# A new hand-written order for gated linear attention with an MLP: two late transposes on TensorE instead of one, one transfer transpose less, 119 fillers dealt out anew

## The chip, the cores and the metric

The kernel runs on one core of a Trainium2 chip. The core has five engines that run side by side, each through its own queue in order: TensorE (PE in the profile; PEld is its loading of weights), VectorE (DVE), ScalarE (ACT), GpSimd (POOL) and SyncE (SP), which here only issues transfers. The metric is the device time of one execution in microseconds. The profile's span, from the first to the last instruction, is a little shorter than that time.

## What is computed

Four batches, 8 heads, 768 steps, head size 48. A state of 48 x 48 complex numbers per head is turned and damped at each step by a gate, takes in the product of k and v, and is read with q. The result, laid out as 384 columns, goes through a LayerNorm, a two-layer MLP with ReLU (384 to 1536 to 384) and a residual.

```python
mag = np.sqrt(a_re * a_re + a_im * a_im)
scale = np.minimum(mag, 0.999) / (mag + 1e-06)
a_re_n, a_im_n = (a_re * scale, a_im * scale)
for t in range(S):
    ar, ai = (a_re_n[:, :, t, :, None].copy(), a_im_n[:, :, t, :, None].copy())
    new_re = ar * S_re - ai * S_im
    new_im = ar * S_im + ai * S_re
    kv = np.einsum('bhd,bhe->bhde', k[:, :, t], v[:, :, t])
    S_re, S_im = (new_re + kv, new_im)
    y[:, :, t] = np.einsum('bhd,bhde->bhe', q[:, :, t], S_re)
...
xn = (x - mu) / np.sqrt(var + 1e-06) * g_ln
ch = np.maximum(xn @ w_ch1, 0.0) @ w_ch2
return (x + ch).astype(np.float32)
```

## The kernel before

The recurrence is worked in chunks of 128 steps. Two neighbouring chunks form a pair; there are 12 pairs (P = 0 to 11, three to a batch) and 24 chunks (n = 2P and 2P + 1). Within a chunk the gates' logarithms and angles are summed up over the steps by a matmul with a triangle of ones, exponentials and sines of the sums scale q and k, and then the chunk is ordinary masked attention plus a carried state.

Each operation has a name, and the program has two parts. The function `pair_ops` (from line 397) only declares the operations: what each emits, which others it needs, which buffers it uses. The order is not worked out by anything: it is written by hand in a table, `PLAN` (line 39). A token is `name:engine`, with the number of the PSUM bank behind the engine where it writes one (`th.5.0:A`, `ph.5.0:P4`), and sometimes `@other`, which makes it wait until `other`, an operation of another engine, is done; line 208 calls this taking turns at the shared port, and it is used on POOL alone. `Graph.run` (line 162) emits the operations in the order of the table. So each engine's queue is the table read for that engine alone, and an operation that waits holds up everything behind it on its engine.

The names, by pair and chunk, with their lines:

- On the gates: `are`, `aim` load the two parts (449). `ln` and `iv` (452, 454) are a logarithm and an exponential of are on ACT; `r` (456) is the ratio aim/are on DVE or POOL; `r2` (460) its square, on ACT, DVE or POOL; `u` (466) the logarithm of 1 + r2 on ACT; `l` and `lc` (469, 473) sum and clip on DVE; `th` (489) the arctangent on ACT.
- The sums over steps on PE: `dec` (477, matmuls on 481) from `lc`, and `ph` (492, 507; pair 0 on 511 and 515) from `th` and from `car` (522), the angle carried from the pair ahead.
- From these on ACT: `e`, `en` (484, exponentials of dec), `sin` (533), `cos` (544, 556). `tab.log` and `tab.trig` (815) load one or the other table of functions into ACT.
- The factors: `ke`, `qe` (562) and `ks`, `qs` (572) are products on DVE or POOL.
- The transposes of ks and qs, one for each chunk, reach `ksT` and `qsT` in one of two ways (line 610 to 631): on PE (`kT`, `qT`, eight matmuls with the identity, line 613) and a copy from PSUM on DVE or ACT, or by a transfer that transposes, issued by SP (line 618). Where the table puts `ksT.n:S`, there is no `kT.n`.
- The attention: `am` (636) the scores, `atm` (644) the mask, `gm` and `G` (657, 673) the carried state, `y` (683) the output, `x` (695) its copy.
- The MLP: `bn` and `rstd` (698, 720) the statistics, `xtr` and `xT` (704, 711) the transpose of x, `mm1` (737), `relu` (752), `mm2` (771), `oa` and `ot` (779, 784), and `st` (796) the store. `wl.0` to `wl.5` (367) load the weights through POOL's queue, `wp` (386) and `wc` (391) fold LayerNorm's mean and gain into the first weight matrix. `v` (413) is a cast of the loaded `vf`.
- `dps`, `decc` (589, 599) bring the chunk's total decay to where the state needs it.

Pair 0 is cut into two halves of four heads each (`PARTS`), so its operations have a last index 0 or 1 and 384 columns instead of 768.

The fillers `warmw` (512 columns) and `warm` (256 columns) are matmuls whose results nobody reads; 119 of them stand in the table up to the first chunks' attention. They give PE something to run where it would wait for the gates.

Of the kernel before, what the change touches and what calls it, by code (L numbers as in the profile page):

```python
# [44 lines left out]
k.1.0:S warmw.12:P0 warmw.13:P0 warmw.14:P0 warmw.15:P0 warmw.16:P0 warmw.17:P0 warmw.18:P0 warmw.19:P0 warm.0:P0
warm.1:P0 warm.2:P0 warm.3:P0 warm.4:P0 warm.5:P0 warm.6:P0 warm.7:P0 warm.8:P0 warm.9:P0 warm.10:P0 warm.11:P0
warm.12:P0 warm.13:P0 warm.14:P0 warm.15:P0 warm.16:P0 warm.17:P0 warm.18:P0 dec.0.1:P5 en.0.1:A5 e.0.1:A5 iv.2.0:A
q.1.1:S l.1.0:V lc.1.0:V warm.19:P0 warm.20:P0 warm.21:P0 warm.22:P0 warm.23:P0 warm.24:P0 warm.25:P0 warm.26:P0
warm.27:P0 warm.28:P0 warm.29:P0 dps.0:P5 dec.1.0:P1 q.1.0:S pad.e.1:G@lc.0.0 are.3.0:S en.1.0:A1 vf.0.0:S
cmean:G@l.1.0 decc.0:V5 r.2.0:V wl.1:G e.1.0:A1 warm.30:P0 warm.31:P0 warm.32:P0 warm.33:P0 warm.34:P0 warm.35:P0  # L50
warm.36:P0 warm.37:P0 warm.38:P0 warm.39:P0 warm.40:P0 warm.41:P0 warm.42:P0 warm.43:P0 warm.44:P0 dps.1:P7 qrow:G
r2.2.0:V vf.0.1:S ke.0.0.0:V u.2.0:A wgc:V pad.ks.1:G@uth aim.3.0:S tab.trig.1:A qe.0.1.0:V th.0.1:A l.2.0:V car0.1:G
k.1.1:S warm.45:P0 warm.46:P0 warm.47:P0 warm.48:P0 warm.49:P0 warm.50:P0 warm.51:P0 warm.52:P0 warm.53:P0 warm.54:P0
warm.55:P0 warm.56:P0 warm.57:P0 warm.58:P0 warm.59:P0 warm.60:P0 warm.61:P0 warm.62:P0 warm.63:P0 ph.0.1:P2
qe.0.0.0:V th.0.0:A pad.ks.0:G ke.0.1.0:V pad.qs.1:G@ke.0.0.0 sin.0.1:A2 qs.0.1.1:V car.0.1:A2 ph.0.0:P5 vf.1.1:S
k.2.1:S vf.1.0:S are.4.0:S q.2.1:S warm.64:P0 warm.65:P0 warm.66:P0 qt.0.1:P2 th.1.0:A lc.2.0:V wl.0:G car.0.0:V5
sin.0.0:A5 wp.1:P3 decc.1:V7 ks.0.1.1:V warm.67:P0 warm.68:P0 warm.69:P0 warm.70:P0 qt.0.0:P5 wc.1.1:V3 ks.0.0.1:V
cos.0.1:A2 ph.1.0:P6 th.2.0:A ke.1.0.0:G@qs.0.1.1 wc.1.0:V3 wc.1.2:V3 sin.1.0:A6 qe.1.0.1:G cos.0.0:A5 warm.71:P0
warm.72:P0 warm.73:P0 warm.74:P0 warm.75:P0 warm.76:P0 warm.77:P0 warm.78:P0 warm.79:P0 warm.80:P0 warm.81:P0
# [1 line left out]
q.2.0:S qs.0.1.0:V ln.3.0:A wc.0.0:V1 wc.0.1:V1 qe.1.0.0:G qs.1.0.1:G@car.1.0 e.2.0:A4 ksT.0:A3 wl.2:G@car.1.0
iv.3.0:A warm.83:P0 warm.84:P0 warm.85:P0 warm.86:P0 warm.87:P0 warm.88:P0 warm.89:P0 warm.90:P0 warm.91:P0 warm.92:P0
warm.93:P0 warm.94:P0 warm.95:P0 warm.96:P0 qT.1:P5 qT.0:P2 v.0:G wc.0.2:V1 qsT.0:V2 qsT.1:V5 qt.1.0:P6 kT.1:P3
k.2.0:S tab.trig.3:A am.0:P0 ksT.1:V3 warm.97:P2 ph.2.0:P4 atm.0:V0 cos.1.0:A6 ke.1.0.1:G@qsT.0 r.3.0:G am.1:P2
gm.0:P7 sin.2.0:A4 y.0:P6 qt.2.0:P4 atm.1:V2 qs.1.0.0:V ks.1.0.0:V ks.1.0.1:V G.0:A7 gm.1:P7 x.0:A6 cos.2.0:A4
warm.98:P1 xtr.0:P0 r2.3.0:A y.1:P3 qT.3:P1 qT.2:P5 xT.0:V0 kT.3:P2 x.1:A3 qsT.3:V1 qsT.2:A5 kT.2:P3 th.3.0:A
tab.log.4:A xtr.1:P0 wl.3:G@qsT.3 ksT.3:V2 wp.2:P6 xT.1:V0 v.1:G@xT.1 ksT.2:V3 am.3:P4 u.3.0:A G.1:V7 ln.4.0:A
mm1.0.0.1:P0 ke.2.0.1:G@ksT.2 gm.2:P7 mm1.0.0.0:P0 aim.4.0:S G.2:A7 atm.3:V4 mm1.0.1.1:P2 wc.2.0:V6 qe.2.0.1:G@atm.3
wc.2.1:V6 am.2:P4 qe.2.0.0:G wc.2.2:V6 vf.2.1:S relu.0.0:A0 pad.ks.2:G@wc.2.0 are.5.0:S atm.2:V4 wl.4:G@wc.2.1
mm1.0.1.0:P2 gm.3:P7 relu.0.1:A2 q.3.1:S vf.2.0:S q.3.0:S iv.4.0:A y.3:P6 x.3:V6 ke.2.0.0:G k.3.0:S G.3:V7 ph.3.0:P0  # L70
y.2:P2 car.3.0:V0 mm1.0.2.1:P4 x.2:A2 xtr.3:P3 qs.2.0.1:V xT.3:V3 r.4.0:G@car.3.0 bn.1:V wl.5:G k.3.1:S xtr.2:P7
xT.2:A7 mm1.0.2.0:P4 mm1.1.1.0:P2 mm1.1.1.1:P2 tab.trig.5:A sin.3.0:A0 relu.1.1:A2 aim.6.0:S relu.0.2:V4 mm1.1.2.1:P6
bn.0:V mm1.1.2.0:P6 are.6.0:S qs.2.0.0:V mm2.0.0:P5 aim.5.0:S abs.3.0:A0 l.3.0:V r2.4.0:V lc.3.0:V th.4.0:A
mm1.1.0.0:P3 qT.4:P0 qT.5:P1 mm2.0.1:P5 cos.3.0:A relu.1.2:V6 qsT.5:V1 ks.2.0.1:G@r2.4.0 bn.3:V mm2.1.0:P2 vf.3.0:S
# [772 lines left out]
```

## Time and profile before

| | |
|---|---|
| time, median of 3 runs (lowest to highest) | 188.53 us (188.46 to 189.46) |
| time of the profiled execution | 188.47 us |
| its span | 186.8 us |
| granted TensorE clock, mean | 1.00 |
| transfers in the span | 36.98 MB, 198 GB/s on average |

How such a profile is read: busy times are sums over the span for each engine. A timeline row gives the start, how long the instruction (or a run of like ones) takes, the engine, the line of the kernel, what it writes and reads, and, in brackets, how long the engine had been idle before it and what ended that. A row of the groups gives a count, the busy time and mean time of one, and the idle time before them. The chain of waits is followed back from the last instruction, and tells at each moment which engine's work or which wait set the end. SPq is SP's queue of transfers; a transfer's time runs from its issue to its landing.

### The profile page before, as it was taken

The numbers are of one execution on the slowest core, as the hardware profiler recorded it, in microseconds if no ns is written. First come the engines' busy times: TensorE is split into PE (matmuls) and PEld (weight loads), VectorE is DVE, ScalarE is ACT, GpSimd is POOL, SyncE is SP. The second block draws the span as 40 slices with busy tenths as digits, with TensorE's granted clock in tenths as the row PEclk, the third lists the DMA queues.
The fourth block names the chain that finished last, engine by engine and source line by source line (L and its number), as shares of the span: only waits on it lengthen the run. The fifth ranks groups of instructions, "written<-read, shape, count | busy, mean of one in ns | idle before, by whom it ended". The sixth has DMA issues, their size and how long they took to land.

```text
span 186.8 us, 5174 instructions
## 1 busy us (share of the span) xinstructions
PE 179.2 (96%) x2046; PEld 138.6 (74%) x2048; DVE 154.4 (83%) x277; ACT 158.9 (85%) x225; POOL 120.3 (64%) x131
## 2 busy tenths in 40 slices
PE   5999999999999999999999999999999999799992
PEld 2488777887777889667877887878868778587771
DVE  0789999999999989979898899989999797465421
ACT  4879999998999999999999999998999788356530
POOL 8256647585706994187899991848997938474230
PEclk9999999999999999999999999999999999999999
DMA  5999989899999999879999996999989899996222
GB/s 128 297 251 184 251 197 197 173 221 237 214 246 239 192 284 234 176 136 213 219 264 208 238 261 141 197 194 186 218 154 186 194 212 148 224 132 230 75 84 86
DMA packets 130744, 36.98 MB, mean 198 GB/s; under 512 B 124832, under 2 KB 130720, under 8 KB 130720
## 3 DMA queue, kind: packets, MB, share of 16 engines
...
q8 instruction: 16, 0.26, 0.6%
...
## 4 chain that ended last, share of the span: by engine, by line
PE 71%; DMA 3%; DVE 1%; SPq 1%; issue 0%; DVEq 0%
PE banks L773 25%; PE banks L741 21%; PE banks L636 5%; PE banks L613 4%; PE banks L507 4%; PE banks L481 3%; DMA qsT<-qs 3%; PE banks L686 2%; PE banks L707 2%; PE banks L689 2%; PE banks L664 2%; SPq L618 1%; PE banks L592 1%; PE banks L660 1%; DVE car L528 0%
## 5 line engine op out<-in xcount | busy, mean ns | idle before, releaser
L773 PE MATMUL banks<-w2b,h 128*128 128x384 bf16 (+1 forms) x300 | 54.8, 319 | 0.0
L741 PE MATMUL banks<-xT,w1b 128*128 128x256 bf16 x432 | 51.9, 272 | 0.1
L741 PEld LDWEIGHTS <-w1b 128*128 128x128 bf16 x432 | 41.1, 98 | 6.2 <-DVE xT L290 0.5
L773 PEld LDWEIGHTS <-h 128*128 128x128 bf16 x300 | 26.6, 97 | 12.3 <-ACT h L758 0.3
L293 DVE TENSOR_TENSOR atm<-banks,mask 128x1024 bf16<-128x1024 f32 x24 | 29.0, 1219 | 7.5 <-PE banks L636 7.3
L758 ACT ACTIVATE h<-banks 128x1024 bf16<-128x1024 f32 (+1 forms) x27 | 26.7, 1005 | 5.3 <-PE banks L741 5.1
L293 POOL TENSOR_TENSOR qe<-q,e 128x384 bf16<-128x384 f32 x17 | 18.3, 1080 | 10.2 <-ACT e L485 6.9
L815 ACT ACT_TABLE_LOAD x18 | 23.1, 1283 | 1.1 <-PEq L831 0.8
L293 POOL TENSOR_TENSOR ke<-k,en 128x384 bf16<-128x384 f32 x20 | 18.8, 945 | 6.6 <-DVE qs L293 2.4
L293 POOL TENSOR_TENSOR ks<-ke,trig 128x768 bf16<-128x768 bf16 x13 | 21.2, 1641 | 2.7 <-DVE r L293 2.0
L293 POOL TENSOR_TENSOR r<-aim,are 128x768 f16<-128x768 f32 x7 | 12.9, 1838 | 7.9 <-ACT are L454 4.1
L293 POOL TENSOR_TENSOR qs<-qe,trig 128x768 bf16<-128x768 bf16 x8 | 13.9, 1746 | 6.2 <-DVE car L528 3.4
L636 PE MATMUL banks<-qsT,ksT 128*128 128x128 bf16 x192 | 14.3, 219 | 1.2 <-DMA qsT<-qs 1.2
L636 PEld LDWEIGHTS <-ksT 128*128 128x128 bf16 x192 | 12.3, 97 | 3.3 <-issue 1.3
L786 POOL TENSOR_TENSOR ot<-ot,x 128x384 f32<-128x384 f32 x11 | 11.3, 1038 | 3.2 <-DVE ot L789 1.7
L699 DVE BATCH_NORM_STATS2 stats<-x 128x6 f32<-128x384 bf16 x24 | 13.1, 547 | 0.0
L760 DVE TENSOR_SCALAR h<-banks 128x1024 bf16<-128x1024 f32 (+1 forms) x10 | 11.6, 1159 | 1.6 <-PE banks L741 1.6
L470 DVE SCALAR_TENSOR_TENSOR l<-r,w 128x768 f16<-128x768 f16 (+1 forms) x13 | 11.9, 917 | 0.6 <-ACT r L466 0.6
L806 PE MATMUL banks<-u_e 128*128 128x256 f16 x99 | 12.4, 273 | 0.0
L452 ACT ACTIVATE w<-are 128x768 f32<-128x768 f32 (+1 forms) x13 | 10.3, 791 | 2.4 <-DMA are<-in_a_re_dram 2.4
L686 PE MATMUL banks<-v,atm 128*128 128x48 bf16 x192 | 12.1, 183 | 0.1
L789 DVE SCALAR_TENSOR_TENSOR ot<-banks,rstd,x 128x384 f32<-128x384 f32 (+1 forms) x14 | 8.2, 584 | 4.7 <-PE banks L773 4.3
...
## 6 DMA issues: line engine op xcount, KB each, us to landing
...
```

What stands on the lines that cost most here:

```text
L293: {"DVE": nc.vector, "POOL": nc.gpsimd}[eng(name)].tensor_tensor(**kw)
L470: nc.vector.scalar_tensor_tensor(out=S_("l"), in0=S_("r2"), scalar=0.5, in1=S_("w"), op0=ALU.mult, op1=ALU.add)
L636: nc.tensor.matmul(ps[:, h], lhsT=T("ksT", n)[:, h], rhs=T("qsT", n)[:, h], start=True, stop=True)
L686: nc.tensor.matmul(ps[:, h], lhsT=T("atm", n)[:, h], rhs=T("v", P)[:, c, h], start=True, stop=nfirst)
L699: nc.vector.bn_stats(out=T("stats", n), in_=T("x", n))
L741: nc.tensor.matmul(ps[:, jj], lhsT=w1b[:, dc, ts(gi * JG + jj, C)], rhs=T("xT", P)[:, dc].rearrange("p c t -> p (c t)"), start=(dc == 0), ...
L758: act(out=dst, in_=src, func=AF.Relu)
L760: nc.vector.tensor_scalar(out=dst, in0=src, scalar1=0.0, scalar2=None, op0=ALU.max)
L773: nc.tensor.matmul(bank(own)[:, 0:w], lhsT=T("h", P)[:, j, ts(c, C)], rhs=w2b[:, j, es], start=(j == 0), stop=(j == NJ - 1))
L786: nc.gpsimd.tensor_tensor(out=T("ot", n)[:, es], in0=T("ot", n)[:, es], in1=T("x", n)[:, es], op=ALU.add)
L806: g.add(f"warm.{i}", lambda i=i: nc.tensor.matmul(bank(f"warm.{i}")[:, 0:256], lhsT=u_e[:, 0, 0], rhs=u_e[:, 1].rearrange("p j t -> p (j t ...
L815: g.add(f"tab.{nm}.{i}", lambda tab=tab: nc.scalar.preload_act_table_set(tab))
```

## The change

`PLAN` is replaced by another table of the same operations, in another order, with some of them on other engines. By count, the operations that change their engine are: `r2.0.0`, `r2.0.1`, `r2.1.0` from DVE to ACT, `r2.3.0` and `r2.10.0` from ACT to POOL, `r2.4.0` from DVE to POOL; ten `ks` from POOL to DVE and four from DVE to POOL (13 on DVE before, 19 now); `qs` four from POOL to DVE and five the other way; six `relu` from ACT to DVE and three back; four `G` and four `x` from DVE to ACT, and two `x` and one `G` back; six `xT` from ACT to DVE and one back; `v.2`, `v.3`, `v.5`, `v.6`, `v.9`, `v.10` to POOL, `v.7` to DVE and `v.11` from POOL to ACT; `ksT.2`, `qsT.11`, `qsT.15`, `car.3.0` and three other `car` from DVE to ACT, `car.0.1` and `car.10.0` the other way; and a few `ke`, `qe`, `r`, `rstd`, `abs`, `st`.

The transposes: `qT.19` and `kT.20` are now on PE, with their copies on DVE; `qT.22` goes, and `qsT.22` is a transfer. So there are 21 transfers for ks and qs instead of 22. The marked turns (`@`) are 38 instead of 45. The fillers are 101 narrow and 18 wide instead of 99 and 20. In front of `dec.0.0` stood 12 wide ones; now 18 wide and 30 narrow stand there. `wp.0` is now ahead of `dec.2.0` on PE; before it was behind.

The first rows of the old and of the new table, the rows with the late transposes, and the fillers' loops:

```diff
-tab.log.0:A are.0.0:S ue:G pick:G car0.0:G ln.0.0:A iv.0.0:A aim.0.0:S are.0.1:S mask:G ln.0.1:A r.0.0:V r2.0.0:V
-u.0.0:A gln:S are.1.0:S iv.0.1:A l.0.0:V aim.0.1:S ln.1.0:A lc.0.0:V pad.qs.0:G aim.1.0:S iv.1.0:A are.2.0:S r.0.1:V
-aim.2.0:S r2.0.1:V warmw.0:P0 warmw.1:P0 warmw.2:P0 warmw.3:P0 warmw.4:P0 warmw.5:P0 warmw.6:P0 warmw.7:P0 warmw.8:P0
-warmw.9:P0 warmw.10:P0 warmw.11:P0 dec.0.0:P3 uth:V pad.qs.2:G e.0.0:A3 en.0.0:A3 pad.e.0:G ident:G@r2.0.1
...
-warm.82:P0 dec.2.0:P4 tab.log.2:A en.2.0:A4 qs.0.0.0:V ks.0.0.0:V qs.0.0.1:V wp.0:P1 ks.0.1.0:V car.1.0:V6 kT.0:P3
...
-mm2.17.0:P0 ks.10.0.1:G@ot.15 k.11.1:S tab.log.16:A vf.10.1:S st.9:S k.11.0:S qe.10.0.0:G atm.19:V5 mm2.17.1:P0
-y.18:P2 mm2.17.2:P0 st.11:S dps.10:P6 ksT.21:S vf.10.0:S e.11.0:A3 qs.10.0.0:V x.18:A2 st.12:S y.19:P5 qs.10.0.1:V
-decc.10:V6 qsT.21:S ksT.20:S mm2.16.2:P1 qsT.20:S x.19:V5 xtr.18:P6 xtr.19:P5 xT.18:V6 en.11.0:A3 xT.19:V5 ph.11.0:P2
...
+ue:G ident:G are.0.0:S cmean:G pick:G pad.qs.0:G aim.0.0:S tab.log.0:A ln.0.0:A car0.0:V are.0.1:S iv.0.0:A r.0.0:V
+r2.0.0:A gln:S ln.0.1:A are.1.0:S iv.0.1:A u.0.0:A aim.0.1:S wgc:V ln.1.0:A iv.1.0:A r.0.1:V aim.1.0:S r2.0.1:A uth:V
+are.2.0:S r.1.0:V k.0.0:S aim.2.0:S u.0.1:A r2.1.0:A qrow:G zdec:G q.0.0:S l.0.0:V u.1.0:A pad.ks.1:G l.0.1:V pickf:V
+lc.0.0:V q.0.1:S ln.2.0:A car0.1:G warmw.0:P0 warmw.1:P0 warmw.2:P0 warmw.3:P0 warmw.4:P0 warmw.5:P0 warmw.6:P0
...
+dec.0.0:P5 lc.0.1:V e.0.0:A5 l.1.0:V mask:G@lc.0.0 pad.ks.0:G en.0.0:A5 lc.1.0:V iv.2.0:A r.2.0:V pad.e.0:G@pickf
+wl.1:G@lc.1.0 k.0.1:S dec.0.1:P6 warm.30:P0 warm.31:P0 warm.32:P0 warm.33:P0 warm.34:P0 warm.35:P0 warm.36:P0
+warm.37:P0 dec.1.0:P2 pad.e.1:G@lc.1.0 r2.2.0:V e.0.1:A6 wl.0:G@r.2.0 pad.qs.1:G@r.1.0 k.1.0:S e.1.0:A2 en.1.0:A2
...
+wp.0:P4 qs.0.0.0:V dec.2.0:P2 qe.1.0.1:G sin.1.0:A6 ks.0.0.0:V tab.log.2:A warm.82:P0 warm.83:P0 qT.1:P1 are.3.0:S
+qT.0:P5 wc.0.1:V4 ks.0.1.0:V car.1.0:V6 e.2.0:A2 en.2.0:A2 qsT.1:V1 vf.0.0:S vf.0.1:S warm.84:P0 warm.85:P0 warm.86:P0
...
+mm1.8.1.0:P4 mm1.8.0.0:P0 l.11.0:V mm1.8.1.1:P4 sin.10.0:A2 qsT.18:S ke.10.0.0:G@xT.17 mm1.8.0.1:P0 k.11.1:S
+ke.10.0.1:G v.9:G ot.11:G relu.8.1:V4 oa.14:A7 ot.15:V6 qT.19:P7 relu.8.0:A0 ksT.19:S bn.16:V lc.11.0:V mm1.8.2.0:P2
...
+en.11.0:A2 dps.10:P5 tab.trig.17:A x.18:A7 y.19:P6 decc.10:V5 xtr.18:P2 th.11.0:A x.19:A6 mm2.16.2:P1 xT.18:V2 st.11:S
+kT.20:P5 qs.10.0.0:V ksT.21:S xtr.19:P6 ph.11.0:P2 ksT.20:V5 G.19:V4 ot.16:V1 xT.19:A6 qs.10.0.1:G mm1.9.1.0:P6
+qsT.21:S oa.17:A0 sin.11.0:A2 ot.17:G mm1.9.1.1:P6 abs.11.0:A2 v.10:G mm1.9.0.1:P4 mm1.9.0.0:P4 mm1.9.2.1:P2
+mm1.9.2.0:P2 ke.11.0.1:V relu.9.1:V6 ke.11.0.0:V bn.19:V qsT.20:S q.11.1:S qe.11.0.1:G@ke.11.0.1 cos.11.0:A gm.20:P6
...
-    for i in range(99):
+    for i in range(101):
         g.add(f"warm.{i}", lambda i=i: nc.tensor.matmul(
...
-    for i in range(20):
+    for i in range(18):
         g.add(f"warmw.{i}", lambda i=i: nc.tensor.matmul(
```

More of the change, by code (lines that the diff above doesn't have):

```diff
@@ L45 @@
[L45 to L59, printed above, removed]
@@ L60 @@
-warm.82:P0 dec.2.0:P4 tab.log.2:A en.2.0:A4 qs.0.0.0:V ks.0.0.0:V qs.0.0.1:V wp.0:P1 ks.0.1.0:V car.1.0:V6 kT.0:P3
[L61 to L74, printed above, removed]
@@ new lines @@
+mm1.1.0.0:P2 bn.3:V mm1.1.0.1:P2 relu.1.2:V6 vf.2.1:S are.5.0:S qT.4:P5 vf.3.1:S qsT.4:V5 ks.2.0.0:G@lc.3.0 th.4.0:A
+qT.5:P0 aim.5.0:S dec.3.0:P6 bn.0:V qsT.5:V0 relu.1.0:A2 tab.log.6:A mm2.2.0:P3 ks.2.0.1:V e.3.0:A6 r2.4.0:G
+pad.ks.2:G bn.2:V u.4.0:A l.4.0:V mm2.1.1:P4 mm2.0.0:P5 en.3.0:A6 kT.5:P1 mm2.0.1:P5 kT.4:P0 mm2.2.1:P3 qe.3.0.1:V
+ksT.5:A1 qe.3.0.0:G qs.3.0.1:V ke.3.0.0:V ln.6.0:A mm2.3.0:P1 lc.4.0:V rstd.0:A qs.3.0.0:V iv.6.0:A mm2.0.2:P5
+rstd.1:A dec.4.0:P6 en.4.0:A6 k.4.1:S e.4.0:A6 aim.6.0:S ke.3.0.1:G@qs.3.0.0 dps.3:P2 ks.3.0.0:G ksT.4:V0 mm2.2.2:P3
```

147 lines of the change are left out of this document (82 added, 65 removed).

## The prediction

> **What bounds the kernel now.** First the busy times of the page, then a table of six stretches, cut where ScalarE (ACT) hands over to TensorE (PE), then the two engines' own rows there.
>
> ```profile
> PE 179.2 (96%) x2046; PEld 138.6 (74%) x2048; DVE 154.4 (83%) x277; ACT 158.9 (85%) x225; POOL 120.3 (64%) x131
> ...
> core 0: us, PE busy (x) PEld busy (x) DVE busy (x) ACT busy (x) POOL busy (x), PEclk, DMA share, GB/s
> 0.00:17.00 17.00, 14.78 (x106) 9.48 (x107) 10.41 (x24) 12.80 (x20) 9.95 (x32) 1.00 0.96 216
> 17.00:43.00 26.00, 25.64 (x325) 20.75 (x325) 25.61 (x47) 24.67 (x36) 15.37 (x17) 1.00 1.07 207
> 43.00:65.30 22.30, 22.23 (x267) 17.14 (x266) 22.04 (x44) 22.07 (x31) 13.92 (x12) 1.00 1.09 227
> 65.30:152.50 87.20, 87.15 (x1021) 67.76 (x1021) 80.33 (x137) 83.84 (x118) 67.08 (x55) 1.00 0.97 205
> 152.50:165.00 12.50, 11.31 (x139) 8.99 (x138) 7.67 (x14) 7.09 (x11) 6.90 (x7) 1.00 1.21 197
> 165.00:186.80 21.80, 18.06 (x196) 14.42 (x193) 8.35 (x16) 8.46 (x12) 7.07 (x10) 1.00 0.46 116
> ```
>
> PE looks like the bound everywhere, but up to 32 us its busy time holds 119 fillers, which only use up time in which PE would wait. The engine that paces the front is ACT: from 17 to 65.3 us it is busy 46.7 of 48.3 us. DVE is as dense in the third stretch (22.04 of 22.30). After 65.3 PE has one visible hole. The handover:
>
> ```profile
> 64.42 0.85 ACT L489 ACTIVATE th<-r 128x768 f16<-128x768 f16 x1
> ...
> 65.29 0.04 issue
> 65.33 1.14 PE banks L507 x6
> ```
>
> th.5.0 ends on ACT at 65.27, and its reader ph.5.0 starts on PE at 65.33. So the span is a sum over this point: ACT's work up to th.5.0, 12.80 + 24.67 + 22.07 = **59.5**; ACT's idle time before it, 65.3 - 59.5 = **5.8**; PE's work from ph.5.0 on, 87.15 + 11.31 + 18.06 = **116.5**; and what is left, 186.8 - 65.3 - 116.5 = **5.0**, which is PE's waits and the last output's way out. Of these 5.0 one wait is named:
>
> ```profile
> 151.74 1.32 SPq L618 DMA_TRANSPOSE qsT<-qs  x1
> 153.10 1.34 SPq L618 DMA_TRANSPOSE ksT<-ks  x1
> 154.49 1.57 SPq L618 DMA_TRANSPOSE qsT<-qs  x1
> ...
> 154.49 5.64 DMA qsT<-qs
> ...
> 160.17 0.61 PE L636 MATMUL banks<-qsT,ksT 128*128 128x128 bf16 x8 [1.19 <-DMA qsT<-qs]
> ```
>
> SP issues qsT.21, ksT.20 and qsT.20 one behind the other; the last lands 5.64 us after its issue, and am.20 with all of PE behind it stands 1.19 us. So 3.8 of the 5.0 stay at the end in any order.
>
> **The change part by part.** The same sum for the new table.
>
> *ACT's work up to th.5.0.* Read off the two tables, ACT gets there, in addition, r2.0.0, r2.0.1, r2.1.0 (from DVE), ksT.2 (from DVE), car.3.0 and car.0.0 (from DVE) and rstd.1 (from POOL); it loses car.0.1, r2.3.0, v.3 and xT.2. car.0.0 against car.0.1 and r2.1.0 against r2.3.0 are of one size and cancel.
>
> ```profile
> L525 ACT ACTIVATE car<-banks 32x384 f16<-32x384 int16 x3 | 1.4, 482 | 0.0
> L288 ACT COPY ksT<-banks 128x1024 bf16<-128x1024 bf16 x2 | 2.0, 1025 | 0.0
> L466 ACT ACTIVATE r<-r 128x384 f16<-128x384 f16 x2 | 1.0, 523 | 0.0
> L724 ACT ACTIVATE rstd<-rstd 128x2 f32<-128x2 f32 x6 | 1.2, 203 | 0.2
> L416 ACT CAST v<-vf 128x768 bf16<-128x768 f32 x4 | 3.3, 828 | 0.3 <-DMA vf<-in_v_dram 0.3
> L288 ACT COPY xT<-banks 128x384 bf16<-128x384 bf16 x8 | 3.9, 481 | 1.1 <-PE banks L707 1.0
> ```
>
> A Square on 384 columns isn't shown; the Ln on 384 (523 ns) is the nearest row. So 2 x 0.52 + 1.03 + 0.48 + 2 x 0.20 - 0.83 - 0.48 = 1.64; successive rows overlap a little, and I take **+1.5**.
>
> *ACT's idle time before th.5.0.* This is where the new table can win.
>
> ```profile
> 0.79 1.28 ACT L815 ACT_TABLE_LOAD   x1 [0.79 <-PEq L831]
> 3.52 0.52 ACT L452 ACTIVATE w<-are 128x384 f32<-128x384 f32 x1 [1.44 <-DMA are<-in_a_re_dram]
> 5.16 0.52 ACT L452 ACTIVATE w<-are 128x384 f32<-128x384 f32 x1 [0.56 <-DMA are<-in_a_re_dram]
> 6.90 0.84 ACT L452 ACTIVATE w<-are 128x768 f32<-128x768 f32 x1 [0.35 <-DMA are<-in_a_re_dram]
> 10.38 0.84 ACT L466 ACTIVATE r<-r 128x768 f16<-128x768 f16 x1 [0.59 <-DVE r L293]
> 13.83 0.81 ACT L485 ACTIVATE en<-banks 128x768 bf16<-128x768 f32 x1 [0.38 <-PE banks L481]
> ...
> 42.59 0.48 ACT L288 COPY xT<-banks 128x384 bf16<-128x384 bf16 x1 [0.51 <-PE banks L707]
> ...
> 4.63 0.56 DVE L293 TENSOR_TENSOR r<-aim,are 128x384 f16<-128x384 f32 x1 [4.63 <-ACT are L454]
> ```
>
> The first two (2.23) stay, since the first loads are the same. The next four, 1.88, are waits for the loads of are, for DVE's square and for PE's dec.1.0. With the squares on ACT itself the loads have landed by the time that it asks for them, and nothing waits for DVE's square. In their place r2.0.0 waits for r.0.0, which DVE runs from 4.63 to 5.19: ACT is free at 4.6, so 0.65 new. One more new wait comes from the fillers:
>
> ```profile
> 2.22 5.01 PE L810 MATMUL banks<-u_e 128*128 128x512 f16 x12 [2.22 <-POOL u_e L322]
> 7.08 0.49 PE L481 MATMUL banks<-l,u_e 128*128 128x192 f16 x4
> 7.40 1.89 PE L810 MATMUL banks<-u_e 128*128 128x512 f16 x8
> 9.13 2.24 PE L806 MATMUL banks<-u_e 128*128 128x256 f16 x19
> 11.20 0.49 PE L481 MATMUL banks<-l,u_e 128*128 128x192 f16 x4
> ```
>
> Now 12 wide fillers stand ahead of dec.0.0, then 18 wide and 30 narrow. Twelve take 4.86 us from start to start, six more (9.13 - 7.40)/8 = 0.216 each, 1.3, and 30 at (11.20 - 9.13)/19 = 0.109, 3.3: dec.0.0 starts at 11.7 instead of 7.1 and is out at 12.1. ACT reaches e.0.0 after a table load and thirteen operations, eight of them on 384 columns: 2.23 + 0.65 + 1.28 + 8 x 0.52 + 5 x 0.84 = 12.5, less some 0.05 for each that starts before the one ahead of it has ended, 11.9. So 0.25 there, bounded by 0 (ACT later than I think) and 0.8 (a slower start of PE). xT.2 leaves ACT, and with it the 0.51. What stays unnamed in the three stretches (0.1 + 0.8 + 0.2, less what is named in the second one) is some 0.6; I add 0.3 for what I can't see. 2.23 + 0.65 + 0.25 + 0.6 + 0.3 = **4.0** against 5.8. Below 3.1 it can't go (2.23 + 0.65 + what is left of the 0.25); above, it is open, and that is the slow rival.
>
> *PE's work from ph.5.0 on.* kT.20 and qT.19 come, qT.22 goes: one group of eight transposes more. The two fillers more and two wide ones fewer all lie in the head, ahead of the point, and are hidden beneath ACT.
>
> ```profile
> 60.11 0.45 PE banks L613 x8
> ```
>
> **+0.45**, 117.0. Their two copies go to DVE, which is free for 6.9 us of the stretch up to 152.5 and for 4.8 of the next, so they are hidden; if DVE were full at that moment they would cost some 0.7 each (a copy of the same size takes ACT 1.03).
>
> *PE's waits after it.* kT.20 takes ksT.20 out of SP's queue, so qsT.20 follows qsT.21 directly, 1.4 us sooner against a wait of 1.19. qs.10.0.1 moves to POOL for it, behind two products; if POOL is late, both transposes and the loads queued behind them on SP are. I take 0.2 of the 1.19, ends 0 and 1.2. The two transposes back on SP (qsT.22, and the earlier place of qsT.23) have over a us of room.
>
> *Moves that I cost at nothing.* DVE loses some 3.5 us of work ahead of th.5.0 (three squares, car, ksT.2, v.2, qe.3.0.0), so its dense stretch gets slack. POOL, busy 13.9 of 22.3 there, takes v.2, v.3, r2.4.0. The changed turns between them add waits on POOL alone: wl.1 behind lc.1.0, wl.0 behind r.2.0; behind these stand pad.qs.1 and ke.1.0.0.
>
> *Sum:* 59.5 + 1.5 + 4.0 + 117.0 + 0.2 + 3.8 = **186.0** against 186.8. The profiled execution took 188.47, 1.67 more than its span; the median shown is 188.53, the same within 0.1. 186.0 + 1.67 = **187.7 us**, 0.4% less.
>
> **The rivals.** 0.5% (0.94 us: below 187.6, above 189.5) is about what a measurement tells from no change.
>
> *Cleaner than that.* ACT's idle is 3.4, nothing waits late: 187.7 - 0.6 - 0.2 = 186.9. For it: DVE no longer paces together with ACT. Against it: each front order has small holes that nobody names.
>
> *The port turns against it.* DVE's products and POOL's hold each other up:
>
> ```profile
> L293 DVE TENSOR_TENSOR ks<-ke,trig x13: 346/554/1915, 20.5 to 147.6; 128x768 bf16<-128x768 bf16 x9, 128x384 bf16<-128x384 bf16 x4
> ```
>
> The same product takes 0.55 us mostly and 1.9 once. The new table has 19 of them on DVE instead of 13, and 38 marked turns instead of 45. One such collision ahead of th.5.0 costs 1.4, of which DVE's new slack and ACT's order hide perhaps a third: 187.7 + 0.9 = 188.6. Against it: POOL has six ks fewer. The Trainium skill, SBUF — State Buffer, section Who interferes with whom, says that a DVE instruction with two SBUF inputs and a GpSimd instruction that reads SBUF exclude each other for the whole instruction. The trace agrees with the 1.9.
>
> *Slower: dec.2.0 behind a weight load.* The new order puts wp.0 ahead of dec.2.0 on PE, and wp.0 waits for wl.0.
>
> ```profile
> 16.36 0.79 POOL L368 DMA_DIRECT2D w1b<-in_moe_w_ch_dram  x1
> ...
> 23.39 1.28 ACT L815 ACT_TABLE_LOAD   x1
> ...
> DMA to landing us min/median/max: 5.8/6.7/7.7
> ```
>
> wl.0 now stands behind r.2.0 on DVE, which waits for iv.2.0 on ACT (done by about 13.7 if e.0.0 starts at 12.1); so it is issued at about 14.8 instead of 16.36, and by the slowest, 7.7, lands at 22.5. e.2.0 is the first that ACT does after the table load at 23.39: the three squares put that off by some 1.9, the vanished waits bring most of it back, so ACT asks at about 25. wp.0 and dec.2.0 are three and four matmuls, 1.5 with their way out by the row of the 512-wide fillers (0.216 each): the load is late from 23.5 on, and from there each us of it is a us of ACT, which has none to give back up to 65.3. Landed at 24.3 the kernel is level with before; at 25.4 it takes 187.7 + 1.9 = 189.6. Against it: that would be over 10 us from the issue, and none of the three took that long. For it: DMA is at 0.96 to 1.07 of its engines in these stretches.
>
> **How the numbers follow.** Forecast 0.48 (187.2 to 188.4, nearly half of it below 187.6: 0.22), cleaner 0.20, port 0.17, weight load 0.15. Faster 0.20 + 0.22 = 0.42; within 0.26 + 0.17 = 0.43; slower 0.15. The range runs from 186.4 (ACT's idle at its floor, 3.1; no late wait; 0.2 less work on ACT where rows overlap more: 187.7 - 0.9 - 0.2 - 0.2) to 189.3 (a collision, 0.9, and most of the late wait, 0.7).
>
> **What would show it.** th.5.0 ending near 65.0 with ACT busy some 61 us before it shows the first two terms; r2.0.0 waiting 0.6 for DVE and e.0.0 0.2 for PE the new waits; am.20 starting with no wait for a transfer the fourth. A wait of e.2.0 for PE, PE's wp standing for a load, or a ks on DVE over 1.5 us ahead of 65 would show a rival. The forecast is wrong if ACT's idle before th.5.0 is above 5.

## The result, and the profile after

The new table is slower: 189.53 us median (188.85 to 191.14) against 188.25 us (187.89 to 189.46) of the kernel before beside it, a ratio of 1.0067 with a 95% interval of 1.0048 to 1.0087. 187.7 was forecast. The profiled execution took 190.56 us, with a span of 188.4; it is one of the longer ones (the median of the 15 spans is 187.3; the profiled execution of the kernel before has 186.8), so single traces are read here with care, and where it matters several are put side by side.

First the busy times, from the page of the new kernel, and the same six stretches as before (the last one ends with the longer span); the columns are those of the table in the prediction.

```profile
PE 179.2 (95%) x2056; PEld 138.9 (74%) x2056; DVE 154.1 (82%) x275; ACT 159.1 (84%) x228; POOL 114.6 (61%) x131
...
core 0: us, PE busy (x) PEld busy (x) DVE busy (x) ACT busy (x) POOL busy (x), PEclk, DMA share, GB/s
0.00:17.00 17.00, 14.38 (x98) 9.49 (x99) 8.92 (x19) 13.42 (x22) 9.73 (x30) 1.00 0.94 216
17.00:43.00 26.00, 23.75 (x316) 19.42 (x314) 24.83 (x46) 24.78 (x35) 14.85 (x16) 1.00 1.05 198
43.00:65.30 22.30, 22.01 (x265) 16.92 (x263) 20.80 (x38) 21.73 (x31) 16.48 (x15) 1.00 1.10 223
65.30:152.50 87.20, 86.93 (x1021) 67.99 (x1019) 78.03 (x133) 82.88 (x119) 59.59 (x55) 1.00 0.99 200
152.50:165.00 12.50, 12.40 (x174) 10.06 (x171) 10.74 (x20) 8.48 (x14) 6.07 (x6) 1.00 1.12 194
165.00:188.40 23.40, 19.71 (x200) 15.04 (x198) 10.75 (x20) 7.80 (x11) 7.90 (x12) 0.99 0.54 129
```

PE's busy time is the same 179.2, so the 1.6 us of span are time in which PE waits, and the second row has them: 2.25 us of 26 without work, where before there were 0.36. The next view is what PE waited for (in total, times, longest), and under it the rows of the timeline around the two longest waits, from PE, ACT and POOL, and the row that gives the landing times of the weight loads.

```profile
PE banks L388 <- DMA w1b<-in_moe_w_ch_dram: 1.8, 2, 1.1
...
21.19 0.81 PE L388 MATMUL banks<-w1b,gc 128*128 128x512 bf16 x3 [0.65 <-DMA w1b<-in_moe_w_ch_dram]
24.77 0.82 PE L388 MATMUL banks<-w1b,gc 128*128 128x512 bf16 x3 [1.14 <-DMA w1b<-in_moe_w_ch_dram]
25.43 0.81 PE L481 MATMUL banks<-l,u_e 128*128 128x384 f16 x4
...
24.17 1.28 ACT L815 ACT_TABLE_LOAD   x1
26.28 0.81 ACT L485 ACTIVATE e<-banks 128x768 bf16<-128x768 f32 x1 [0.83 <-PE banks L481]
...
14.11 1.00 POOL L368 DMA_DIRECT2D w1b<-in_moe_w_ch_dram  x1 [0.53 <-DVE l L473]
15.39 0.79 POOL L368 DMA_DIRECT2D w1b<-in_moe_w_ch_dram  x1
...
DMA to landing us min/median/max: 6.4/7.0/9.3
```

This is the slow rival of the prediction. wp.0 (24.77) stands 1.14 us for wl.0, issued at 15.39 and landed 9.3 later; dec.2.0 (25.43) comes behind it; and e.2.0, the first that ACT does after its table load, stands 0.83 us for dec.2.0. th.5.0 ends at 66.8 instead of 65.3.

The late part reads differently. From PE's timeline:

```profile
105.63 0.34 PE L707 MATMUL banks<-ident,x 128*128 128x128 bf16 x3 [0.20 <-ACT x L288]
...
161.05 0.61 PE L636 MATMUL banks<-qsT,ksT 128*128 128x128 bf16 x8
...
168.08 0.36 PE L664 MATMUL banks<-v,ks 128*128 128x48 bf16 x8 [0.32 <-ACT v L416]
```

am.20 (161.05) has no wait any more, as forecast. But PE now stands at several other places for 0.1 to 0.5 us, among them xtr.10 for the copy of x on ACT, and gm.22 for v.11, which moved from POOL to ACT. From ph.5.0 to PE's last matmul it takes 118.05 us, against 117.73 before.

### The profile page after: what moved, and what is told of

Its sections match the earlier page's. It is cut to its first block, busy times and chain, and to the rows that moved or that the text cites. A ratio compares the mean times of both kernels' runs of the same rounds, so it can differ in the third digit from the quotient of the medians.

```text
span 188.4 us, 5181 instructions
## 1 busy us (share of the span) xinstructions
PE 179.2 (95%) x2056; PEld 138.9 (74%) x2056; DVE 154.1 (82%) x275; ACT 159.1 (84%) x228; POOL 114.6 (61%) x131
## 4 chain that ended last, share of the span: by engine, by line
PE 59%; ACT 17%; DMA 10%; DVE 4%; issue 3%; POOL 3%; SPq 2%; ACTq 0%; DVEq 0%
PE banks L741 16%; PE banks L773 16%; PE banks L613 5%; DMA w1b<-in_moe_w_ch_dram 5%; PE banks L636 5%; ACT L815 4%; PE banks L507 4%; PE banks L481 3%; DMA aim<-in_a_im_dram 3%; DMA vf<-in_v_dram 2%; PE banks L686 2%; POOL ot L786 2%; PE banks L664 2%; ACT h L758 2%; PE banks L689 2%
## 5 line engine op out<-in xcount | busy, mean ns | idle before, releaser
L773 PE MATMUL banks<-w2b,h 128*128 128x384 bf16 (+1 forms) x300 | 55.5, 319 | 0.2
L741 PE MATMUL banks<-xT,w1b 128*128 128x256 bf16 x432 | 51.0, 272 | 0.0
L758 ACT ACTIVATE h<-banks 128x1024 bf16<-128x1024 f32 (+1 forms) x24 | 23.6, 1008 | 4.5 <-PE banks L741 3.0
L293 POOL TENSOR_TENSOR ke<-k,en 128x384 bf16<-128x384 f32 x18 | 17.2, 956 | 15.0 <-ACT car L525 5.7
L760 DVE TENSOR_SCALAR h<-banks 128x1024 bf16<-128x1024 f32 (+1 forms) x13 | 15.2, 1175 | 6.6 <-PE banks L741 6.5
L786 POOL TENSOR_TENSOR ot<-ot,x 128x384 f32<-128x384 f32 x11 | 9.9, 912 | 8.5 <-ACT ot L779 8.4
L293 POOL TENSOR_TENSOR qs<-qe,trig 128x768 bf16<-128x768 bf16 x9 | 14.7, 1642 | 0.4
L293 POOL TENSOR_TENSOR r<-aim,are 128x768 f16<-128x768 f32 x6 | 11.6, 1931 | 4.6 <-ACT are L454 4.6
L470 DVE SCALAR_TENSOR_TENSOR l<-r,w 128x768 f16<-128x768 f16 (+1 forms) x13 | 12.9, 996 | 1.7 <-ACT r L466 1.6
L293 POOL TENSOR_TENSOR ks<-ke,trig 128x768 bf16<-128x768 bf16 x7 | 11.4, 1642 | 1.4 <-DVE l L473 1.0
```

The source lines that it names most:

```text
L293: {"DVE": nc.vector, "POOL": nc.gpsimd}[eng(name)].tensor_tensor(**kw)
L470: nc.vector.scalar_tensor_tensor(out=S_("l"), in0=S_("r2"), scalar=0.5, in1=S_("w"), op0=ALU.mult, op1=ALU.add)
L741: nc.tensor.matmul(ps[:, jj], lhsT=w1b[:, dc, ts(gi * JG + jj, C)], rhs=T("xT", P)[:, dc].rearrange("p c t -> p (c t)"), start=(dc == 0), ...
L758: act(out=dst, in_=src, func=AF.Relu)
L760: nc.vector.tensor_scalar(out=dst, in0=src, scalar1=0.0, scalar2=None, op0=ALU.max)
L773: nc.tensor.matmul(bank(own)[:, 0:w], lhsT=T("h", P)[:, j, ts(c, C)], rhs=w2b[:, j, es], start=(j == 0), stop=(j == NJ - 1))
```

## The experiments

All of them keep the whole computation. Each ratio is to executions of the kernel before on the same chip. "Diff" lines are tokens of the table.

**dec_first**: only the order on PE.

```diff
-wp.0:P4 qs.0.0.0:V dec.2.0:P2 qe.1.0.1:G
+dec.2.0:P2 wp.0:P4 qs.0.0.0:V qe.1.0.1:G
```

> The new table with one token moved: dec.2.0 stands ahead of wp.0 again, as before the change. Theory L (the late load): in the new kernel's trace PE stands 1.14 us for wl.0 at wp.0, dec.2.0 comes behind it and ACT waits 0.83 us for it at e.2.0; with dec.2.0 ahead that wait goes, th.5.0 ends about 0.8 sooner (66.0) and the median falls from 189.5 to about 188.7. Rival A (ACT's own work): the loss up to th.5.0 is the work that ACT took over (three squares, a copy), ACT is dense behind e.2.0 and simply finds another wait; the median stays at 189.3 to 189.6. Rival P (PE is the bound from here on): wp.0 stands as long as before, only four matmuls (0.65) slip into its wait; the gain is 0.65 at most.

Measured: 1.0073 (1.0046 to 1.0100), no gain. Its trace tells why, in PE's and ACT's timelines:

```profile
23.10 0.81 PE L481 MATMUL banks<-l,u_e 128*128 128x384 f16 x4
24.82 0.82 PE L388 MATMUL banks<-w1b,gc 128*128 128x512 bf16 x3 [0.91 <-DMA w1b<-in_moe_w_ch_dram]
...
25.29 0.81 ACT L485 ACTIVATE e<-banks 128x768 bf16<-128x768 f32 x1
...
28.00 1.01 ACT L288 COPY ksT<-banks 128x1024 bf16<-128x1024 bf16 x1 [0.47 <-PE banks L613]
```

ACT's wait at e.2.0 is gone, as theory L had it, but wp.0 is as late as ever, and everything on PE behind it with it. ACT now stands 0.47 us at ksT.0, the copy of what kT.0 writes on PE behind wp.0, and ph.5.0 starts 41.62 us behind wp.0, at 66.44. The order alone can't mend it.

**wl_early**: the loads issued earlier.

```diff
-mask:G@lc.0.0 ... wl.1:G@lc.1.0 ... wl.0:G@r.2.0
+wl.1:G@lc.0.0 wl.0:G mask:G
```

> The new table, but POOL issues wl.1 and wl.0 ahead of mask (at about 11.7 and 12.5 us instead of 14.1 and 15.4). Theory L: both land 2 us sooner or more, PE's two waits at wp.1 and wp.0 (0.65 and 1.14 us) go, e.2.0 does not wait, and the median falls from 189.5 to 188.7 or, if PE itself sets the end from there on, to 187.8. Rival A: no gain, 189.3 to 189.6. Rival Q (the transfers share the rate of all loads): landing times move by less than 1 us, or the loads of k, q and are land later in exchange, and the median stays above 189.0.

Measured: 1.0051 (1.0027 to 1.0076). In the trace wl.0, issued at 13.46, landed at 22.33, PE no longer waits for the loads, and ph.5.0 starts at 65.96; the gain, some 0.3 us by the two ratios, is smaller than L said, and not clear of the noise.

**wp_first**: the table of before, with the new order of the two.

```diff
-dec.2.0:P4 tab.log.2:A en.2.0:A4 qs.0.0.0:V ks.0.0.0:V qs.0.0.1:V wp.0:P1
+wp.0:P1 dec.2.0:P4 tab.log.2:A en.2.0:A4 qs.0.0.0:V ks.0.0.0:V qs.0.0.1:V
```

> The table of before with one token moved: wp.0 stands ahead of dec.2.0, as in the new one. Theory L: wl.0 lands at 24.1 us there, so dec.2.0 moves from 23.3 to about 24.8 and en.2.0, the first to read it on ACT, from about 24.7 to 25.6: the median rises from 188.25 to about 189.1. Rival A: ACT has fewer squares there, but if its order decides and not this wait, 188.2 to 188.5. Rival P: PE loses the time that it stands for the load with nothing to do in it, at most 0.65: up to 188.9.

Measured: 1.0024 (1.0005 to 1.0044): slower, by half of what L said (by 0.1 to 0.8 us, with the interval). wl.0 landed at 23.57 there, earlier than in the trace of before, dec.2.0 started at 24.25, and en.2.0 on ACT stood 0.29 us for it.

**r2_dve**: the three squares back on DVE.

```diff
-r2.0.0:A ... r2.0.1:A ... r2.1.0:A
+r2.0.0:V ... r2.0.1:V ... r2.1.0:V
```

> The new table with the three squares r2.0.0, r2.0.1 and r2.1.0 back on DVE (1.9 us of work less on ACT, 1.0 more on DVE). Rival A: ACT reaches th.5.0 some 1.5 us sooner and the median falls from 189.5 to about 188.0. Theory L: ACT gets to e.2.0 sooner but finds dec.2.0 behind the same load, and waits there instead: the median stays within 189.2 to 189.6. My prediction's own sum: the squares only fill what would be waits for loads and for DVE, so within 0.3 of 189.5 too.

Measured: 1.0090 (1.0062 to 1.0118). Rival A falls: ACT has 1.5 to 1.7 us less to do ahead of th.5.0 than in the traces of the new front, and it brings nothing. ACT's idle time there is 6.75 us instead of 4.4 to 5.5, and PE stands 0.7 us for wl.0 as before. The median is above what L and my own sum said, 0.4 us by the ratio, with intervals that overlap.

**front_new, rest_new, front28_old**: one table up to a cut, and behind it the operations that are left in the order of the other.

```diff
-(front_new) the table of before up to ph.5.0
+(front_new) the new table up to ph.5.0
...
-(rest_new) the operations left behind ph.5.0, in the order of before
+(rest_new) the same in the new order
```

front28_old is rest_new with the cut at tab.trig.3 (28.6 us).

> The new table up to ph.5.0 and, behind it, the operations that are then left in the order of before. Theory F (the loss is in the front): ph.5.0 starts at 66 to 67 instead of 65.3, and the median is 0.7 to 0.8 above before's 188.4, 189.1 to 189.2, plus whatever of the 0.5 outside the span belongs to the front. Theory R (the rest is where the forecast gain is missing, the front costs nothing): 188.2 to 188.6. My prediction's terms: 0.3 less in the front, 188.1.

> The table of before up to ph.5.0 and, behind it, the operations that are then left in the new order, with both late transposes on TensorE. My prediction's terms for this part: 0.45 more matmul work, 1.0 less of the wait for the transfer, so 187.8. Theory F: the same, 187.8 to 188.2, since the rest is not where the loss is. Theory R: 188.8 or more. If the time outside the span (1.7 in before, 2.2 in the new kernel) is 2.2 here, it belongs to the rest of the table; if 1.7, to the front.

> The table of before up to tab.trig.3 (28.6 us) and, behind it, the new order. Theory F with its cause in the head (three squares more on ACT, dec.0.0 late, the wait at e.2.0): all of that is gone, so as rest_new, 187.8 to 188.2. If the front loses between 28 and 65 us instead (ksT.2, car.3.0, rstd.1 on ACT): as front_new, 189.1 or more.

Measured: 1.0033 (1.0003 to 1.0063), 1.0077 (1.0042 to 1.0112), 1.0058 (1.0029 to 1.0086). The three don't add up: by front_new the front costs 0.6 us, by rest_new the rest more than the whole change. In rest_new's trace ph.5.0 starts at 66.38 and PE needs 119.38 us from there, 1.3 more than in the new kernel: its seam is bad, so it says little. Each order is fitted to itself; a cut through it is a new kernel. front28_old keeps the old order of dec.2.0 and of the weight loads, and its ph.5.0 starts at 65.97; 187.8 to 188.2 was expected of it if the loss came from the head, and at 1.0058 most of the loss is still there. What the three do say: both parts lose something.

**late_transpose, late_transpose2**: the late transpose on TensorE alone, in the table of before; first behind xtr.19 with bank 2, then behind mm1.9.1.0 with bank 5.

```diff
-ksT.20:S
+kT.20:P2 ... ksT.20:V2    (late_transpose)
+kT.20:P5 ... ksT.20:V5    (late_transpose2)
```

> The table of before with one part of the change: kT.20 on TensorE (behind xtr.19) and ksT.20 copied by DVE instead of the transfer. My prediction's term: matmul work 0.45 more, the wait of am.20 for qsT.20 (1.19 us in the first trace of before, 0.55 in the trace of wp_first) down to 0.2 or less: 187.8 to 188.3. Rival: the wait is taken over by gm.21, y.21 or another transfer, and the 0.45 are a plain loss: 188.7 to 188.9.

> As late_transpose, but kT.20 and its copy use bank 5 and stand four microseconds later on TensorE, behind mm1.9.1.0: in late_transpose they shared bank 2 with ph.11.0, which then stood 0.85 us for the copy. My prediction's term: 0.45 more matmul work, against a wait of am.20 of 0.5 to 1.2 us that goes: the median 0 to 0.7 us below before. Rival (the wait is taken over by another operation): 0.2 to 0.5 us above before.

Measured: 1.0033 (1.0006 to 1.0059), and 0.9989 (0.9976 to 1.0002). The first one made a wait of its own, the row of ph.11.0 in PE's timeline:

```profile
153.64 0.81 PE L507 MATMUL banks<-th,u_th 128*128 128x384 f16 x4 [0.85 <-DVE ksT L290]
```

ph.11.0 writes to the bank that ksT.20 is still copied from. With another bank the wait is gone and so is that of am.20: the transpose by itself is worth some 0.2 us at the ratio measured, with an interval that reaches from 0.5 us to nothing.

**act_less**: ksT.2 and car.3.0 back on DVE, rstd.1 on POOL.

```diff
-ksT.2:A2 ... car.3.0:A0 ... rstd.1:A
+ksT.2:V2 ... car.3.0:V0 ... rstd.1:G
```

> The new table with ksT.2 and car.3.0 on DVE and rstd.1 on POOL, as before the change: 1.9 us of work less on ACT ahead of th.5.0, in the stretch where ACT has hardly a hole. My prediction's model (ACT paces the front): th.5.0 1.0 to 1.9 us sooner and the median from 189.6 to 188.2 or so. Rival P (PE, with its fillers, paces the front from 25 us on): less than 0.3 us. Rival D (DVE is the one that is late): 0 or a loss.

Measured: 1.0113 (1.0091 to 1.0136). ACT's waits between 30 and 67 us in its trace (in total, times, longest):

```profile
ACT h L758 <- PE banks L741: 1.0, 2, 0.6
ACT G L288 <- PE banks L664: 0.7, 1, 0.7
ACT en L485 <- PE banks L481: 0.4, 1, 0.4
ACT x L288 <- PE banks L689: 0.4, 1, 0.4
```

ACT has 1.7 us less to do ahead of th.5.0 than in the first trace of the new kernel and idles 2.0 more, and ph.5.0 starts at 67.37. So the model by which ACT paces the front, and which had 188.2 here, fails; "0 or a loss" is what came. The rows show ACT standing for PE; that DVE, with more to do, held PE up is my reading and was not tried.

**few_fill**: the 19 fillers behind wp.0 left out (warm.82 to warm.100).

> The new table without the 19 fillers behind wp.0 (from 25.6 us on, 19 x 0.109 = 2.1 us of TensorE). My prediction's model: they only use up time in which PE would wait for ACT; the median stays at 189.3 to 189.8, with PE's idle time up by 2 us. Rival P: PE is late itself from wp.0's wait on and the fillers are in the way; the median falls by 0.8 to 2 us, to 187.6 to 188.8.

Measured: 1.0113 (1.0085 to 1.0140), above both expectations and the same as the new kernel itself in a later measurement on another chip (1.0106, below). In the front the fillers are as free as I had said: ph.5.0 starts 42.00 us behind wp.0, with them 42.12 to 42.26. The trace is longer at another place, seen in PE's and POOL's waits (POOL's from 140 to 160 us):

```profile
PE banks L636 <- DMA qsT<-qs: 1.7, 2, 1.0
...
POOL qe L293 <- DMA q<-in_q_dram: 3.5, 1, 3.5
```

The loads of q.10 took 5.5 us instead of 3.5 to 4.5; qe.10 and qs.10.0.1 on POOL were late by that, with them qsT.21 and qsT.20, and am.20 stood 0.97 us (am.22 the other 0.76, for qsT.22). So the late chain can decide; late_v tries it.

**pool_pad**: 8 memsets of 128x80 more on POOL, behind car0.1.

> The new table with 8 small memsets more on POOL at 6.4 us, where it stands idle until 11.7: 206 instructions there, as before the change (205; the new table has 198). Only the time outside the span is looked at: 1.7 in the kernels with 205 to 210 instructions on POOL, 2.0 to 2.3 in those with 195 to 199. If POOL's count of instructions sets it, 1.7 here; if it is something else (SP's count, the order at the end), 2.2.

One execution: 189.02 us, of which 1.92 lie outside the span. That is between the two values expected; after_pads takes it up.

**after_again, late_v, after_pads, late2_pads**, on one chip. after_again is the new kernel as it is.

```diff
-qs.10.0.0:V ... qs.10.0.1:G                     (late_v)
+qs.10.0.0:V qs.10.0.1:V
...
+car0.1:G padx.0:G ... padx.7:G                  (after_pads; late2_pads: six, behind pad.e.0)
+xT.22:S glnx.0:S ... glnx.4:S                   (after_pads)
```

> The new kernel, unchanged, beside the next three. If few_fill and act_less were slower than it by their edits, it stands at 1.005 to 1.009 of before here; if this chip makes the new table slower as a whole, at 1.011.

> The new table with qs.10.0.1 on DVE, behind qs.10.0.0, as before the change (0.55 us there, 1.64 on POOL behind two products). Theory S (the late chain through POOL is what is left of the wait): qsT.21 is issued about 1 us sooner, the small waits around am.20, am.21 and behind them go, and the median is 0.4 to 0.8 below after_again. Rival (it is just in time, as in the first trace, and the loss lies ahead of it): within 0.2 of after_again.

> The new kernel with 8 small memsets more on POOL at 6.4 us and 5 loads of 1.5 KB more on SP behind xT.22 (about 175 us), which do nothing for the result: 206 instructions on POOL and 210 on SP instead of 198 and 205. If the counts set the end (the streams of instructions are fetched in pieces, and a piece is due at the end), the time from the last matmul to the end of the execution falls from 5.5 to 5.1 and the median by 0.3 to 0.4. Rival: only the border of the span moves; the median stays within 0.15 of after_again.

> late_transpose2 (0.9989 of before) with 6 small memsets more on POOL at about 5 us, 211 instructions there: if the count sets the end, 0.35 less again, 0.997 of before (0.9955 to 0.9985). Rival: 0.9989 as without them.

Measured: 1.0106 (1.0063 to 1.0149), 1.0061 (1.0041 to 1.0082), 1.0181 (1.0145 to 1.0217), 0.9978 (0.9961 to 0.9995).

late_v is 0.5 us below after_again by the medians, with intervals that overlap. 0.3 of it is the end alone (table below), and in its trace ph.5.0 to the last matmul takes 117.86, no less than the others. So the chain through POOL is just in time most often; that it costs something at times, as in few_fill, is seen, that it is the loss is not.

after_pads lost 1.4 us against after_again, at the end: issuing its small loads (384 pieces of 4 bytes each) takes SP 2.70 us, the stores behind them are issued from 178.23 on instead of 175.73, and ACT stands for a store that has to free its buffer, as the row of its timeline shows:

```profile
181.09 0.58 ACT L784 ACTIVATE ot<-banks,rstd 128x384 f32<-128x384 f32 x1 [5.08 <-DMA out_dram<-ot]
```

What it was made for, it shows all the same. The time from PE's last matmul to the end of the execution (the profiled execution's own time less PE's last end), beside the number of instructions that the trace records on POOL:

```
before, wp_first, late_transpose, late_transpose2   POOL 202        5.41 to 5.46 us
after, after_again, dec_first, wl_early, r2_dve,
  few_fill                                          POOL 195        5.47 to 5.52
act_less                                            POOL 197        5.57
front28_old                                         POOL 196        5.65
rest_new, late_v                                    POOL 192, 193   5.31, 5.22
front_new, pool_pad, combo_front, late2_pads        POOL 203 to 208 5.05 to 5.23
after_pads, late2_pads2                             POOL 203, 208   4.74, 4.82
```

Where POOL has 197 to 202 records, there is a gap of 0.37 to 0.39 us ahead of the 197th, inside the last 1.1 us, when all else waits for POOL (in before: 196th at 185.67, 197th at 186.04). With 203 or more, the 197th falls into the wait for the last store and the gap costs nothing; with 196 or fewer it isn't in the span, and the time outside the span is up to 0.6 longer instead. So the new kernel's end moved 0.47 from inside to outside, and only 0.07 of it is loss. The Trainium skill, Runtime: NRT & Kernel Launch, section Instruction fetch mechanics, says that an engine's instructions are fetched in blocks of 256 and that crossing a block's border is mostly hidden. A gap at the same record in all five kernels that have 197 to 202 agrees with the blocks; hidden it is not where it comes last. That it is a fetch is my reading; the trace doesn't name it.

**combo_front, late2_pads2.** combo_front is wl_early, dec_first and the 8 memsets together. late2_pads2 is late2_pads with five loads of 4 bytes on SP behind xT.22.

> The new table with wl.1 and wl.0 issued at about 12.5 and 13.5 us (as wl_early), dec.2.0 ahead of wp.0 (as dec_first) and 8 small memsets more on POOL (as pool_pad, worth 0.2). Theory L (the late load is the whole loss of the front): neither dec.2.0 nor wp.0 is late, ACT alone sets the front, ph.5.0 starts at 65.3 to 65.8 us as in the kernel before, and the median is 0.9 to 1.0 below the new kernel's: 0.9995 to 1.002 of before, with the 0.4 us of the rest still there. Rival A (ACT's own work of 1.9 us more): ph.5.0 at 66.3 or later, 1.004 or more.

> late2_pads (0.9978 of before) with 5 loads of 4 bytes more on SP at about 173 us, where SP stands idle for 5 us. In the trace of after_pads SP went through one semaphore wait at the end instead of six, and the end stood 0.92 us behind the last landing instead of 1.21. If that carries over, 0.3 us less: 0.9962 of before. Rival: the loads cost what they save, 0.9975 to 0.9985.

Measured: 1.0038 (1.0007 to 1.0069) and 0.9952 (0.9922 to 0.9982). combo_front's PE and ACT (the line numbers are two higher there):

```profile
22.81 0.81 PE L483 MATMUL banks<-l,u_e 128*128 128x384 f16 x4
23.46 0.81 PE L390 MATMUL banks<-w1b,gc 128*128 128x512 bf16 x3
...
25.07 0.81 ACT L487 ACTIVATE e<-banks 128x768 bf16<-128x768 f32 x1
```

Neither wp.0 nor e.2.0 waits, ACT has 1.5 us more of work than in before, and ph.5.0 starts at 65.56, where L put it and rival A did not. The median came out above what I had expected for it (by 0.2% at least); its executions spread widely, 186.5 to 188.9 in span, and the interval reaches down to the expectation. So that the late load costs the front time is shown by the traces; how much of the median it is, only roughly.

late2_pads2 is 0.7 us below the kernel before by the medians, 187.90 against 188.64, 0.9 by the ratio, and the fastest of all: the late transpose on a bank of its own, and an end that is 0.6 shorter. SP goes through one wait on a semaphore there after the last landing instead of five in before and six in the new kernel, at 0.06 us each.

## Why the prediction was wrong

**What sets ph.5.0.** Read in the traces of all kernels whose front is untouched (idle memsets on POOL aside), in us:

```
                 wl.1 issued  landed   wl.0 issued  landed   dec.2.0   ph.5.0   between
old front
before              12.63     19.31      16.36      24.10     23.28    65.33    42.05
late_transpose      13.17     19.44      16.91      24.09     23.83    65.90    42.06
late_transpose2     13.02     19.14      16.75      23.57     23.69    65.74    42.06
late2_pads          13.18     19.73      16.91      24.75     23.85    65.89    42.05
rest_new            13.04     19.82      16.78      24.27     23.71    66.38    42.67
late2_pads2         12.99     19.27      16.73      23.14     23.65    66.91    43.26
new front
after               14.11     21.15      15.39      24.73     25.43    67.03    41.60
after_again         14.15     21.21      15.43      24.10     24.80    66.27    41.47
front_new           14.08     20.84      15.36      24.49     25.19    66.66    41.46
pool_pad            14.06     20.07      15.34      23.61     24.31    65.78    41.47
late_v              14.67     21.76      15.95      24.86     25.56    67.03    41.46
after_pads          14.48     20.55      15.76      24.28     24.98    66.45    41.46
```

In the new front dec.2.0 starts 0.70 behind the landing of wl.0, each time, and ph.5.0 41.5 to 41.6 behind dec.2.0, each time. The landing of one weight load sets the front. (In pool_pad, where it lands earliest, the chain of waits runs through ACT instead, which is free for the copy ksT.0 no sooner than PE has it ready: there the two tie.) In the old one dec.2.0 doesn't wait for it, and it may land anywhere from 23.14 to 24.75. There ph.5.0 comes 42.05 behind dec.2.0 in four traces of six. In the other two another weight load is late: in late2_pads2 PE stands 1.14 us at wp.2 for wl.2, in rest_new 0.52 us at an mm2 for a load of the second weights. So the old front isn't safe from a late load either; both are traces of executions above their kernel's median (188.77 against 187.90, 191.07 against 189.76). The mean start of ph.5.0 is 65.7 in the four, 66.0 in the six, and 66.5 with the new front. Against the four, dec.2.0 is 1.4 later, and the way from it to ph.5.0 is 0.6 shorter.

How the load gets to ph.5.0 is seen in the chain of waits of after_again (each piece starts where the one before it ends):

```profile
15.43 8.67 DMA w1b<-in_moe_w_ch_dram
24.10 0.05 issue
24.15 0.82 PE banks L388 x3
24.97 0.65 PE banks L481 x4
...
27.49 0.46 PE banks L613 x8
27.95 0.02 issue
27.98 1.01 ACT ksT L288
...
53.73 0.91 ACT ksT L288
54.64 0.04 issue
54.69 1.46 PE banks L773 x8
...
66.27 0.17 PE banks L707 x3
66.43 0.99 PE banks L507 x6
```

wl.0 holds up wp.0, dec.2.0 and kT.0 on PE, ACT stands for kT.0 at the copy ksT.0, and from 54.69 on the chain is PE's own work with no wait over 0.1 us. th.5.0 is not on it: it ends at 66.02 and ph.5.0 starts at 66.27, when PE gets to it; the distance is 0.25 to 0.26 in all six traces of the new front, and 0.05 in the old. So the point at which the prediction cut its sum hands nothing over in the new order. The prediction had put PE's busy time in the front down to the fillers; but these end at 32 us, and in its own table PE is busy for 22.23 of the 22.30 us from 43 to 65.3.

**The sum of the loss.** 0.5 to 0.8 in the front, by the six or the four traces; from ph.5.0 to the last matmul 117.9 (median of nine kernels with the new rest) against 117.1 and 117.7 in the two with the old one, 0.5 more; 0.07 at the end. Together 1.1 to 1.4, against 1.3 measured. It is a sum over single executions. By the medians the late load is worth less: wl_early, combo_front and front28_old, in which it holds up nothing, start ph.5.0 at 65.56 to 65.97 and still take 1.0038 to 1.0058 of before, 0.2 to 0.5 us under the 1.0067 of the new kernel, with intervals that overlap it. So the cause of the late front is shown, and its share of the loss, by these figures, is 0.2 to 0.8 us of the 1.3.

Step by step:

- *ACT's work up to th.5.0, +1.5*: it was +1.6 to +1.9 in the new traces. A little short, and of little weight: r2_dve took as much away again and gained nothing.
- *ACT's idle time, 5.8 to 4.0*: this is the step that failed, and with it the path that it belongs to, on which ACT alone paces the front. It came out at 4.4 to 5.5 (5.38 in the first trace, above the 5 that the prediction had named as its sign of being wrong). The first part was right: r2.0.0 waits 0.63 for DVE (0.65 forecast), and e.0.0 waits for nothing (0.25 forecast; ACT gets there at 12.51, and dec.0.0 is out at 12.24). The waits for the later loads of are are gone in the first trace, and one of them is back, with 0.2 to 0.5, in three of the other five. What I left out of the sum is the late wl.0, which stops PE at wp.0 in all six traces, by 0.46 to 1.22 us, and ACT behind it, by 0.83 at e.2.0 in the first trace and 0.15 in after_again's. I had it as a rival with 0.15, by the right mechanism. The time from which the load is late, 23.5, was right too: wp.0 begins to wait at 23.63 in the first trace, and at 23.2 to 24.2 in the others. Two things were wrong. I let wl.0 take at most 7.7 us from its own issue, so that it landed at 22.5. But in the new front it is issued 1.3 us behind wl.1 and lands 2.9 to 3.7 behind it, 8.3 to 9.3 after its issue; and wl.1 is issued 1.5 later than before, behind lc.1.0, a turn that I named and costed at nothing because behind the turns I saw only pad.qs.1 and ke.1.0.0. With both loads 1.6 to 2.4 earlier (wl_early, combo_front) wl.0 lands at 22.33 and 21.72 and holds up nothing; no run moved wl.1 alone. And a landing at 24.3, which I had put level with the kernel before, is 0.8 late: by the distances of the table, 0.70 and 41.5, ph.5.0 is level with the old 65.7 at a landing of 23.5. The 0.8 that the new order was to gain elsewhere isn't there, for without the late load ph.5.0 starts where the old front has it.
- *PE's work, +0.45*: right. Take for each kind of matmul the usual distance, the median over all traces from its start to the start of the next matmul: from ph.5.0 on these add up to 115.4 us instead of 114.9.
- *PE's waits, 1.0 less*: wrong. am.20's wait (1.35 and 0.71 above the usual distance in before and wp_first) did go. But the sum of all delays above the usual distances is 1.4 to 2.1 in seven traces of the new rest (2.5 in wl_early's, 3.7 in few_fill's), as it is 1.4 and 2.1 in the two of the old one, since some ten small ones have come, at hand-overs of x, v and others from ACT and DVE. So, by these traces, the 0.5 us lost behind ph.5.0 are the transposes' 0.45, with nothing won for them. I had priced the moved transposes and looked at no other hand-over of the 100 us behind ph.5.0. Where only the transpose was moved (late2_pads), the sum is 1.0.
- *The rest of the span, and 1.67 outside it*: from the last matmul on, 3.7 to 3.3 inside and 1.7 to 2.2 outside. Nothing, taken together, but to take either as a constant was luck.
- *The starting point*: the trace of before has the earliest ph.5.0 of its six, 65.33 against a mean of 66.0 (65.7 without the two with a late load). A sum made against one execution has that error from the outset.
- *The port rival*: a ks on DVE took 1.45 us ahead of 65 in the first trace, under the 1.5 named, and 0.94 at most in after_again, pool_pad and late_v. DVE is busy 54.6 us there instead of 58.1. No part of the loss is seen there.
